# Two more attention units by rows, and another spread of the W_o products and second-norm steps over the slots of an iteration

## The chip, the cores and the metric

The kernel runs on one core of one Trainium2 chip. The metric is the device time of one execution in microseconds (us), median of several runs. Engines: PE (TensorE, matmuls), PEld (its weight loads), ACT (ScalarE), DVE (VectorE), POOL (GpSimd), SP (SyncE, which here only issues DMAs).

## The reference

One transformer block on x of 2048 x 512 (batch 1, bf16), with shift, scale and gate vectors from a small conditioning product:

```python
mod = (_silu(c) @ w_mod).reshape(c.shape[0], 6, 1, -1)       # sa, ca, ga, sb, cb, gb
h = _layernorm(x) * (1 + ca) + sa
x = x + ga * attention(h)      # 32 query heads, 8 key/value heads of 128, 2048 cached keys
h = _layernorm(x) * (1 + cb) + sb
x = x + gb * mixer(h)          # gelu(h @ w_in), spatial product over the 2048 rows, gate, w_out
```

The attention is `softmax((h @ wq) k^T / sqrt(128)) v` for every head, then `@ wo`; four query heads share one key/value head (a group). The first norm, the projections and the mixer are small beside the two attention products.

## The kernel before

**Units.** The attention is cut into 128 units (`NU`): unit u is group `u // 16` and tile `u % 16` of 128 rows of x, with the four heads of the group. Every unit has four pieces of work.

- Scores and exponential (`qk`), in iteration u of the main loop. An iteration has eight slots. In each slot PE makes 128 x 1024 scores in one of two PSUM buffers (`s_ps`, two matmuls of 512 columns) and ACT exponentiates them into SBUF.
- Times v (`pv`, `pv_rows`), in iteration `pv_at(u)`.
- Times W_o (`wo_proj`), four matmuls of 512 columns, in iteration `wo_at(u)`; DVE drains them from a PSUM buffer `misc` (two exist, shared with the query projections) and adds them into the tile's `xacc`.
- For the last group (units 112 to 127) the second norm of the finished tile (`ln2`).

**By columns or by rows.** By columns (L1029, L1036) the keys lie on the partitions, the exponentials come out as the stationary operand of the product with v, which then takes 64 matmuls of 129 columns (L1085; the last column sums the softmax's denominator). The result is normalised and transposed by a DMA (`turn`, L1108). By rows (L1010, L1017) the queries lie on the partitions; ACT also sums each row (an accumulator read after each exponential), a DMA transposes each head's 128 x 2048 exponentials into `pT` (`turn_rows`, L1049), and the product with v takes 16 matmuls of 512 columns (L1064). Its result needs no transpose, but each of the four W_o products is drained on its own (L1135), scaled by its head's denominator. The row exponentials lie in six SBUF buffers (three of them in the place of `win_sb`, which is loaded when the last row unit is through).

```python
TURN_A, TURN_B = 2 * CT, NU - CT * 2 - 1     # 8 and 119
LAGS = (2, 3, 1)
def by_rows(u):
    return TURN_A <= u < TURN_B and (u - TURN_A) % len(LAGS) < len(LAGS) - 1
```

So from unit 8 on two of three units go by rows, the third by columns. `LAGS` gives the iterations between a unit's scores and its product with v: 2 and 3 for the two row units, 1 for a column unit, which makes one such product per iteration. `wo_at` adds 3 more, or 2 for the last units.

**The order in a slot** is written out by hand, and each engine works in that order: first what `at(iteration, slot, fn)` has put there (transposes, norm steps, loads), then `qk`, then an eighth of the product with v, then query projections for later units (`fill`: one matmul in each of slots 0 to 3 in most iterations), then a W_o product. W_o products take the last slots:

```python
if i >= NSLOT - len(wf):
    wf[i - NSLOT + len(wf)]()
```

With four of them these are slots 4 to 7; with eight (two units in one iteration) all slots. SP issues its DMAs in program order, so a transpose that waits holds back those behind it.

**Second norm.** After the last W_o product of a tile, POOL (DVE for the last four tiles) applies the gate and adds x. `ln2` then places three steps: statistics on DVE and the reciprocal root on POOL (`first`), normalisation on DVE and a DMA transpose to `xnT` (`second`, L686, L1180), four modulations on DVE into `h2Ts` (`third`, L1187). The mixer's first product (`z2_tile`) reads these tiles from iteration 128 on.

Of the kernel before, what the change touches and what calls it, by code (L numbers as in the profile page):

```python
# [575 lines left out]
def kernel(  # L576
# [23 lines left out]
    REP = HQ // HKV  # L600
# [4 lines left out]
    NT = S // P  # L605
# [4 lines left out]
    CT = 512 // P  # L610
    FC = _f_chunk(FH)
    NFHC = FH // FC
    NSLOT = NKT // 2
# [61 lines left out]
    def rstd_of(mv, n, tag):  # L675

        ve = stat.tile([P, CT], FP32, name=f"ve_{tag}")
        nc.gpsimd.tensor_scalar(
            out=ve[:, :n], in0=mv[:, :, 1], scalar1=LN_EPS, scalar2=None, op0=ALU.add
        )  # L680
        rstd = stat.tile([P, CT], FP32, name=f"rstd_{tag}")
        nc.gpsimd.tensor_tensor(out=rstd[:, :n], in0=ve[:, :n], in1=mhalf[:, :n], op=ALU.pow)
        return rstd

    def normalise(dst, src, mv, rstd):
        nc.vector.tensor_scalar(  # L686
            out=dst,
            in0=src,
            scalar1=mv,
            scalar2=rstd,  # L690
            op0=ALU.subtract,
            op1=ALU.mult,
        )

    def ln_stats(mv, j, src):
        st = stat.tile([P, 1, nc.vector.BN_STATS_DIM], FP32, name="bnst")
        nc.vector.bn_stats(out=st[:, 0, :], in_=src)  # L697
        nc.vector.bn_aggr(out=mv[:, j, :], in_=st[:])
# [97 lines left out]
    def ln1_stats(j0, n):  # L796
        for j in range(j0, j0 + n):
            ln_stats(mv1, j, x_sb[:, j, :])
        return rstd_of(mv1[:, j0 : j0 + n, :], n, "ln1")
# [161 lines left out]
    first = dict(r1=ln1_stats(1, 1))  # L961


    NU = HKV * NT


    TURN_A, TURN_B = 2 * CT, NU - CT * 2 - 1

    LAGS = (2, 3, 1)

    def by_rows(u):
        return TURN_A <= u < TURN_B and (u - TURN_A) % len(LAGS) < len(LAGS) - 1
# [3 lines left out]
    def pv_at(u):  # L976
        return u + (LAGS[(u - TURN_A) % len(LAGS)] if by_rows(u) else 1)

    def wo_at(u):
        return pv_at(u) + (3 if u < NU - 6 else 2)  # L980


    users, homes = dict(pT0=-2, pT1=-1, wsp=TURN_A + 1), {}
# [8 lines left out]
    def at(it, slot, fn):  # L992
        later.setdefault((it, slot), []).append(fn)
# [173 lines left out]
    def ln2(it, j):  # L1167

        st = {}

        def first():
            if j < NT - CT:
                ln_stats(mv2, j, x_sb[:, j, :])
            st["rstd"] = rstd_of(mv2[:, j : j + 1, :], 1, "ln2")

        def second():
            xn = res.tile([P, D], BF16, name="xn2", bufs=2)
            normalise(xn[:], x_sb[:, j, :], mv2[:, j, 0:1], st["rstd"][:, 0:1])
            st["xnT"] = res.tile([P, NDT, P], BF16, name="xnT2", bufs=2)
            nc.sync.dma_start_transpose(out=st["xnT"][:], in_=xn[:])  # L1180

        def third():
            ch, c0 = j // CT, (j % CT) * P
            if ch not in h2Ts:
                h2Ts[ch] = res.tile([P, NDT, 512], BF16, name="hT", bufs=NCH)
            for dt in range(NDT):
                nc.vector.tensor_scalar(  # L1187
                    out=h2Ts[ch][:, dt, c0 : c0 + P],
                    in0=st["xnT"][:, dt, :],
                    scalar1=modc[:, 4 * NDT + dt : 4 * NDT + dt + 1],  # L1190
                    scalar2=modc[:, 3 * NDT + dt : 3 * NDT + dt + 1],
                    op0=ALU.mult,
                    op1=ALU.add,
                )

        at(it + 1, 0 if j >= NT - CT else 3, first)
        at(it + 1, 4 if j >= NT - CT else 5, second)
        at(it + 2, 5, third)

    mod_b = {}  # L1200

# [81 lines left out]
    def set_fill(b):  # L1283


        hole = TURN_A + 1 if (TURN_A + 1) // CT == b - 1 else None
        fs = qproj(b, list(range(REP)), 0, 512)
        for k, fn in enumerate(fs):
            it, slot = (b - 1) * CT + k // NDT, k % NDT
            if hole:  # L1290
                if k < NDT:
                    it, slot = hole - 1, k
                elif k < 3 * NDT:
                    it, slot = hole, k - NDT
                else:
                    it, slot = hole + 1, k - 3 * NDT
            if b == 1:
                it, slot = 2 + (10 + k) // 16, (5 + k // 2) % 8
            elif b == 2:
                it, slot = (5, k // 2) if k < 8 else (it, slot)  # L1300
            fill.setdefault((it, slot), []).append(fn)
# [8 lines left out]
    for g in range(1, HKV):  # L1310
        it = (g - 1) * NT
# [84 lines left out]
    def zrun(n):  # L1396
        for _ in range(min(n, len(zq))):
            zq.pop(0)()
# [13 lines left out]
    def pv_part(u, i, n):  # L1412
        if by_rows(u):
            return pv_rows(u, i, n)
        for k in range(NSLOT // n):
            pv(u, i * (NSLOT // n) + k)

    for it in range(NU + 6):
        if it < NU:
            if it % CT == 0 and it // CT + 1 < NB:  # L1420
                set_fill(it // CT + 1)
        elif it == NU:
            free_a.close()
            z2p = fast.enter_context(tc.tile_pool(name="z2p", bufs=1))
            zs["z2"] = z2p.tile([P, NT, FH], BF16, name="z2")
        pvs = [u for u in range(max(it - 5, 0), min(it, NU)) if pv_at(u) == it]
        wos = [u for u in range(max(it - 8, 0), min(it, NU)) if wo_at(u) == it]
        wf = [fn for u in wos for fn in wo_proj(u)]
        for i in range(NSLOT):
            for fn in later.pop((it, i), []):  # L1430
                fn()
            if it < NU:
                qk(it, i)
            if len(pvs) == 1:
                pv_part(pvs[0], i, NSLOT)
            elif pvs:
                n = NSLOT // 2
                pv_part(pvs[i // n], i % n, n)
            for fn in fill.pop((it, i), []):
                fn()  # L1440
            if i >= NSLOT - len(wf):
                wf[i - NSLOT + len(wf)]()
            if it >= NU:
                zrun(3)
        for u in wos:
            if u >= (HKV - 1) * NT:
                ln2(it, u % NT)
        if it == NU + 2:
            free_b.close()
            mlp = fast.enter_context(tc.tile_pool(name="mlp", bufs=1, side="right"))  # L1450
            zs["z1T"] = mlp.tile([P, NFT, S], BF16, name="z1T")
            wout_sb = mlp.tile([P, NFT, D], BF16, name="wout_sb")
            bsp_bc = mlp.tile([P, S], BF16, name="bsp_bc")
            nc.sync.dma_start(out=wout_sb[:], in_=wout_dram)
            nc.sync.dma_start(out=bsp_bc[:], in_=B_b_sp.partition_broadcast(P))
# [177 lines left out]
```

## Time and profile before

| | |
|---|---|
| median of 3 runs | 1308.32 us (1308.19 to 1308.85) |
| the profiled execution | 1308.74 us, span 1306.8 us |
| granted TensorE clock | 1.0 |
| DMA, share of 16 engines | 83.1% (mostly row transposes) |

The profile page gives the busy time of each engine as a share of the span. Below it are groups of equal instructions (line, engine, operation, output and inputs, shape, count; busy time and mean duration; idle time of the engine before them and who ended it). A timeline row has the start in us from the span's beginning, the duration of one instruction or of several merged ones, the engine, the line, the operation, the count, and in brackets the idle time before it with the instruction that ended it. Matmuls overlap in the pipeline: a row of one 512-column matmul says 0.38 us, while the next starts 0.22 us later, so PE's pace is read from starts.

### The profile page before, as it was taken

Reading aid. Unit: us, or ns where it says so; the run is one execution under the profiler, and the core shown is the slowest. Engines: PE = TensorE matmul, PEld = TensorE weight load, DVE = VectorE, ACT = ScalarE, POOL = GpSimd, SP = SyncE. Lnnn points to the kernel's source line nnn. Section 1 sums busy time; section 2 is a strip of 40 time slices with the busy share of each in tenths; the row PEclk is TensorE's granted clock in tenths of the full one; section 3 lists DMA queues with packets and bytes.
Section 4 is the critical chain, followed back from the end, with each engine's and each line's share of the span. In section 5 each row is a group of like instructions: output and inputs, shape, how many; then the busy total and the mean of one; then the engine's idle time right before and its main releaser. Section 6 shows DMA issues by size and latency. Waiting matters only on the chain.

```text
span 1306.8 us, 22904 instructions
## 1 busy us (share of the span) xinstructions
PE 1298.8 (99%) x8809; PEld 705.7 (54%) x8809; DVE 674.7 (52%) x1740; ACT 1113.5 (85%) x1653; POOL 56.6 (4%) x92
## 2 busy tenths in 40 slices
PE   9999999999999999999999999999999999999998
PEld 5665555555555555555555555555555566644445
DVE  5534445544554455445544554455455657694443
ACT  7899999999999999999999999999999988650000
POOL 1000000000000000000000000000000134210000
PEclk9999999999999999999999999999999999999999
DMA  7469999999999999999999999999999921364300
GB/s 183 125 127 188 163 193 183 190 168 187 189 188 168 192 168 195 177 170 186 189 189 170 187 189 179 180 188 174 182 187 171 166 82 29 57 137 98 78 20 31
DMA packets 743878, 203.33 MB, mean 156 GB/s; under 512 B 728144, under 2 KB 742608, under 8 KB 743760
## 3 DMA queue, kind: packets, MB, share of 16 engines
q1 hardware_dynamic: 741168, 199.55, 83.1%
q10 hardware_dynamic: 2592, 2.23, 0.6%
q8 instruction: 71, 1.16, 0.4%
q14 instruction: 47, 0.39, 0.1%
HBM read 21.37 MB, written 2.10 MB: 18 GB/s over the span
## 4 chain that ended last, share of the span: by engine, by line
PE 92%; DVE 0%; issue 0%
PE o_ps L1064 20%; PE s_ps L1010 19%; PE o_ps L1085 13%; PE s_ps L1029 12%; PE misc L1142 8%; PE misc L946 8%; PE misc L1500 7%; PE s_ps L1335 2%; PE s_ps L1374 2%; PE o_ps L1533 1%; PE s_ps L1533 0%; PE o_ps L856 0%; DVE xacc L1135 0%; DVE tmp L1545 0%; DVE bnst L697 0%; DVE qT L957 0%
## 5 line engine op out<-in xcount | busy, mean ns | idle before, releaser
L1010 PE MATMUL s_ps<-kT,qT 128*128 128x512 bf16 x1184 | 352.1, 379 | 0.2 <-ACT pn L1017 0.2
L1017 ACT ACTIVATE win_sb<-s_ps 128x1024 bf16<-128x1024 f32 x298 | 305.1, 1024 | 3.1 <-ACT win_sb L1017 0.5
L1036 ACT ACTIVATE pT<-s_ps 128x1024 bf16<-128x1024 f32 x256 | 258.8, 1026 | 16.8 <-PE s_ps L1029 4.8
L1064 PE MATMUL o_ps<-pT,v 128*128 128x512 bf16 x896 | 265.8, 379 | 0.0
L1029 PE MATMUL s_ps<-qT,kT 128*128 128x512 bf16 x864 | 256.8, 379 | 0.3 <-ACT pT L1036 0.2
L1135 DVE SCALAR_TENSOR_TENSOR xacc<-misc,rall,xacc 128x512 f32<-128x512 f32 x290 | 217.1, 749 | 55.5 <-PE misc L1142 49.3
L1017 ACT ACTIVATE pn<-s_ps 128x1024 bf16<-128x1024 f32 x196 | 200.7, 1025 | 1.2
L1142 PE MATMUL misc<-wo_g,oT 128*128 128x512 bf16 x512 | 194.0, 379 | 0.6 <-DVE qT L957 0.6
L1064 PEld LDWEIGHTS <-v 128*128 128x128 bf16 x1184 | 115.8, 98 | 139.7
L1036 ACT ACTIVATE wsp<-s_ps 128x1024 bf16<-128x1024 f32 x176 | 179.5, 1024 | 13.4 <-PE s_ps L1029 5.6
L946 PE MATMUL misc<-hT,wq_g 128*128 128x512 bf16 (+2 forms) x528 | 190.7, 371 | 0.1
L1010 PEld LDWEIGHTS <-qT 128*128 128x128 bf16 x1184 | 115.5, 98 | 103.9 <-issue 0.7
L1085 PEld LDWEIGHTS <-pT 128*128 128x128 bf16 x2048 | 136.8, 98 | 59.0
L957 DVE CAST qT<-misc 128x512 bf16<-128x512 f32 x127 | 87.2, 687 | 156.5 <-PE misc L946 156.4
L1085 PE MATMUL o_ps<-v,pT 128*128 128x129 bf16 x2048 | 157.2, 220 | 0.0
L1053 DVE TENSOR_TENSOR tot<-rs 128x1 f32<-128x1 f32 x296 | 46.3, 157 | 165.4 <-ACT win_sb L1017 110.1
L1029 PEld LDWEIGHTS <-kT 128*128 128x128 bf16 x864 | 83.6, 98 | 86.6 <-issue 1.8
L1085 PEld LDWEIGHTS <-wsp 128*128 128x128 bf16 x1408 | 94.3, 98 | 41.5
L1085 PE MATMUL o_ps<-v,wsp 128*128 128x129 bf16 x1408 | 108.5, 220 | 0.0
L1017 ACT ACTIVATE wmod_a<-s_ps 128x1024 bf16<-128x1024 f32 x98 | 100.3, 1024 | 0.3 <-ACT wmod_a L1017 0.3
L1500 PE MATMUL misc<-wsp,z 128*128 128x512 bf16 (+2 forms) x560 | 100.5, 336 | 0.0
L1064 PE MATMUL o_ps<-wsp,v 128*128 128x512 bf16 x288 | 85.7, 379 | 0.0
(107 smaller groups left out, 861.0 us busy)
## 6 DMA issues: line engine op xcount, KB each, us to landing
wo_g<-in_A_wo_dram SPq DMA_DIRECT2D x8, 512.0 KB, 4.7
wq_g<-in_A_wq_dram SPq DMA_DIRECT2D x7, 512.0 KB, 4.4
v<-in_A_v_cache_dram SPq DMA_DIRECT2D x7, 512.0 KB, 4.8
wsp<-in_w_mod_dram SPq DMA_DIRECT2D x1, 2048.0 KB, 8.8
out_dram<-yout ACTq DMA_DIRECT2D x16, 128.0 KB, 1.7
pT<-win_sb SPq DMA_TRANSPOSE x113, 4.8
win_sb<-in_B_w_in_dram SPq DMA_DIRECT2D x1, 1792.0 KB, 7.4
x_sb<-in_A_x_dram SPq DMA_DIRECT2D x3, 512.0 KB, 5.6
```

What stands on the lines that cost most here:

```text
L946: nc.tensor.matmul(ps[0][:, o0 : o0 + n], lhsT=wqs[g][:, dt, hh * DH : (hh + 1) * DH], rhs=hTs[ch][:, dt, c0 : c0 + n], start=(dt == 0), s ...
L957: nc.vector.tensor_copy(out=dst, in_=src)
L1010: nc.tensor.matmul(s_ps[:, c * 512 : (c + 1) * 512], lhsT=qTs[b][:, hh, jj * P : (jj + 1) * P], rhs=groups[g]["kT"][:, k0 : k0 + 512], sta ...
L1017: nc.scalar.activation(out=rows_of(u, hh)[:, half * HK : (half + 1) * HK], in_=s_ps[:], func=ACT.Exp, scale=inv_sqrt_dh, accum_out=rsums[u ...
L1029: nc.tensor.matmul(s_ps[:, h * 512 : (h + 1) * 512].rearrange("p (r q) -> p r q", r=REP), lhsT=groups[g]["kT"][:, kt * P : (kt + 1) * P], ...
L1036: nc.scalar.activation(out=pTs[u][:, 2 * i : 2 * i + 2, :], in_=s_ps[:].rearrange("p (k q) -> p k q", k=2), func=ACT.Exp, scale=inv_sqrt_dh,)
L1053: nc.vector.tensor_tensor(out=tot[:], in0=rs[:, 2 * hh : 2 * hh + 1], in1=rs[:, 2 * hh + 1 : 2 * hh + 2], op=ALU.add)
L1064: nc.tensor.matmul(o_pss[u][:], lhsT=groups[g]["v1"][:, kt, 0:DH], rhs=pTs[u][:, kt, :], start=(kt == 0), stop=(kt == NKT - 1),)
L1085: nc.tensor.matmul(o_ps[:, hh % 2, 0 : DH + 1], lhsT=pTs[u][:, kt, hh * P : (hh + 1) * P], rhs=groups[g]["v1"][:, kt, 0 : DH + 1], start=( ...
L1135: nc.vector.scalar_tensor_tensor(out=xa[:], in0=X_ps[:], scalar=scale, in1=xa[:], op0=ALU.mult, op1=ALU.add)
L1142: nc.tensor.matmul(ps[0][:], lhsT=oTs[u][:, hh, :], rhs=groups[g]["wo"][:, hh, :], start=(hh == 0 or each), stop=(hh == REP - 1 or each),)
L1500: nc.tensor.matmul(g_pss[f][:, :n], lhsT=z2[:, st, f * P : (f + 1) * P], rhs=wsp[t][:, st, c0 : c0 + n], start=(st == 0), stop=(st == NT - ...
```

## The change

Three parts. `TURN_B` becomes 122, so units 119 and 120 go by rows and 121 closes the pattern by columns; the load of `win_sb`, tied to `TURN_B`, moves from iteration 120 to 123, and the iteration with two products with v from 120 to 123. The W_o delay of 3 instead of 2 iterations now holds for units 122 to 124 too. Iterations with four W_o products put them into slots 0, 2, 4, 6; those with eight use all slots as before, and are now iterations 126 (units 120 and 122) and 128 (124 and 125) instead of 123 (117 and 119) and 125 (121 and 122). The three steps of the second norm move to slots 2 (0 for the last four tiles), 4 and 3.

```diff
-    TURN_A, TURN_B = 2 * CT, NU - CT * 2 - 1
+    TURN_A, TURN_B = 2 * CT, NU - 6
...
     def wo_at(u):
-        return pv_at(u) + (3 if u < NU - 6 else 2)
+        return pv_at(u) + (3 if u < NU - 3 else 2)
...
-        at(it + 1, 0 if j >= NT - CT else 3, first)
-        at(it + 1, 4 if j >= NT - CT else 5, second)
-        at(it + 2, 5, third)
+        at(it + 1, 0 if j >= NT - CT else 2, first)
+        at(it + 1, 4, second)
+        at(it + 2, 3, third)
...
-            if i >= NSLOT - len(wf):
-                wf[i - NSLOT + len(wf)]()
+            if len(wf) > REP:
+                wf[i]()
+            elif wf and i % 2 == 0:
+                wf[i // 2]()
```

## The prediction

> **What bounds the kernel now.** I read the page first (shares of busy time), then the timeline of PE and ACT in iterations 8 to 13, 62 to 65 and 116 to 127, then the SP queue. An iteration of the main loop has eight slots; from iteration 8 on three kinds alternate: A and B exponentiate by rows, C by columns (119 is an A, 120 a B, 121 a C if the pattern goes on).
>
> ```profile
> PE 1298.8 (99%) x8809; PEld 705.7 (54%) x8809; DVE 674.7 (52%) x1740; ACT 1113.5 (85%) x1653; POOL 56.6 (4%) x92
> L1085 PEld LDWEIGHTS <-pT 128*128 128x128 bf16 x2048 | 136.8, 98 | 59.0
> ```
>
> PE is busy throughout, so the test is its pace. The PE timeline gives the starts of iterations 62 (A), 63 (B) and 65:
>
> ```profile
> 547.68 0.59 PE L1010 MATMUL s_ps<-kT,qT 128*128 128x512 bf16 x2
> ...
> 556.49 0.59 PE L1010 MATMUL s_ps<-kT,qT 128*128 128x512 bf16 x2
> ...
> 573.75 0.59 PE L1010 MATMUL s_ps<-kT,qT 128*128 128x512 bf16 x2
> ```
>
> A takes 8.81 us, B and C together 17.26, so 8.63 each. B holds 40 products of 512 columns: 0.2158 us from start to start, with no gap. A holds the 64 products of 129 columns of a column unit in place of 16 long ones: 0.0567 us each. The main loop runs at PE's own pace; from start to start the whole trace holds only some 8 us beyond that pace, about 5 of them before 20 us and few later.
>
> What can make PE wait is the pair of score buffers: the scores of slot i+2 go where ACT has read slot i. The PE timeline of iteration 12 (no W_o there, so two slots have only four products), then ACT's:
>
> ```profile
> 117.99 0.59 PE L1010 MATMUL s_ps<-kT,qT 128*128 128x512 bf16 x2
> 118.42 0.59 PE L1064 MATMUL o_ps<-pT,v 128*128 128x512 bf16 x2
> 118.85 0.59 PE L1010 MATMUL s_ps<-kT,qT 128*128 128x512 bf16 x2
> ...
> 121.01 0.59 PE L1010 MATMUL s_ps<-kT,qT 128*128 128x512 bf16 x2
> ```
> ```profile
> 118.67 1.02 ACT L1017 ACTIVATE win_sb<-s_ps 128x1024 bf16<-128x1024 f32 x1
> 119.59 0.19 ACT L1017 ACTIVATION_READ_ACCUMULATOR win_sb<-s_ps 128x1 f32 x1
> 119.68 1.02 ACT L1017 ACTIVATE win_sb<-s_ps 128x1024 bf16<-128x1024 f32 x1
> ...
> 121.70 1.02 ACT L1017 ACTIVATE wmod_a<-s_ps 128x1024 bf16<-128x1024 f32 x1
> ```
>
> A four-product slot lasts 0.86 us (117.99 to 118.85). A fresh row exponential starts 0.68 to 0.69 after its scores do (118.67; 121.01 to 121.70). The next cannot start sooner than 1.01 later (118.67 to 119.68), so a 0.86 slot leaves ACT behind. When it frees the buffer, iteration 9 shows, where ACT is the limit (ACT, then PE):
>
> ```profile
> 91.42 1.02 ACT L1017 ACTIVATE pn<-s_ps 128x1024 bf16<-128x1024 f32 x1
> 92.33 0.20 ACT L1017 ACTIVATION_READ_ACCUMULATOR pn<-s_ps 128x1 f32 x1
> ```
> ```profile
> 92.58 0.59 PE L1010 MATMUL s_ps<-kT,qT 128*128 128x512 bf16 x2 [0.20 <-ACT pn L1017]
> ```
>
> The exponential ends at 92.44, the accumulator read at 92.53, the waiting scores start at 92.58: 0.14 after the exponential ends. A row exponential thus needs 1.02 + 0.14 = 1.16 us from its start to the reuse of its buffer; a column one has no accumulator read.
>
> **The change, part by part.** Times are against the profiled execution, 1308.74 us with a span of 1306.8; the median of the runs is 1308.32, so a difference is carried over to that.
>
> *Two units more by rows (119, 120).* PE: 16 x 0.2158 = 3.45 for 64 x 0.0567 = 3.63, 0.18 less for each, **-0.35 us**. ACT is slower per row exponential, but 1.08 a slot of PE covers 1.00, as in the 37 pairs before. On DVE four W_o products of each are drained one by one (L1135, 749 ns); the old pattern does the same without a wait.
>
> *W_o in slots 0, 2, 4, 6 instead of 4 to 7.* No product more or less, but the slots become uneven. Old B: eight of 1.079. New B: 1.295, 1.079, 1.295, 1.079, 1.079, 0.863, 1.079, 0.863 (query products stay in 0 to 3). Follow ACT in B: slot 5 fresh, 0.69 after its scores; slot 6: 0.69 + 1.01 - 0.86 = 0.84; buffer free at 0.84 + 1.16 = 2.00 after the scores of slot 6; PE wants it after slots 6 and 7, 1.08 + 0.86 = 1.94. PE waits 0.06. In A the short slots are 0.885: 0.69 + 1.01 - 0.885 = 0.815, free at 1.975, wanted at 1.985: no wait, by 0.01. In C the column exponentials can follow each other in 0.90 (their spacing in iteration 4, where ACT is the limit) and have no accumulator read: no wait. B iterations with this pattern: 15, 18, ... 120, that is 36: 36 x 0.06 = **+2.1 us**, with PE as the bound all of it on the path.
>
> The Trainium skill ("ScalarE: Activation LUTs", section "What ACT_TABLE_LOAD costs") says that an activation with immediate scale and bias takes 186 ns + 0.833 ns per element and that those back to back overlap by about 93 ns, an estimate of 0.95 us for 1,024 elements; by it slot 6 would free its buffer in time and this term would be nil. The rows with an accumulator read disagree: 1.01, and 1.00 once behind.
>
> *What the even spread repairs.* Iteration 11 (no query products; row exponentials against four slots of 0.885) runs from 105.46 to 113.67, 8.21 for a PE sum of 7.94; with W_o in every second slot a pair of slots is 1.985 and the same sum gives no wait: -0.27. Iterations 4, 124, 126, 127 likewise lose 0.08 and three times 0.06: -0.25. Iteration 9 is short of PE work either way (waits of 0.46 now, 0.55 by the same recurrence): +0.1. Together **-0.4 us**.
>
> *The double W_o iteration.* Units 117 and 119 both project in iteration 123 today, together with query products that hold a bank:
>
> ```profile
> 1087.61 0.62 PE L1085 MATMUL o_ps<-v,pT 128*128 128x129 bf16 x8
> 1088.80 0.38 PE L1142 MATMUL misc<-wo_g,oT 128*128 128x512 bf16 x1 [0.57 <-DVE qT L957]
> ```
>
> The product was due at 1087.61 + 8 x 0.057 = 1088.07 and starts 0.73 late; another at 1083.02 is 0.16 late. In the new order the doubles are in 126 and 128, which have no query products: **-0.9 us**.
>
> *Second norm.* Statistics one slot earlier (3 to 2), normalisation and its transpose on SP 5 to 4, modulation 5 to 3. Nothing is added; DVE has slack (52% busy), and PE needs only its drained banks. Behind a waiting DVE stand the drains, due about 0.7 to 1 us before PE would notice. The statistics wait for POOL (1.27 + 1.17); the last W_o product also comes a slot earlier, so cover shifts with need. The modulation waits for xnT: issued at 1036.91 in iteration 118, now ahead of one row transpose, some 2.6 us earlier, landing (2.7 median) near 1037.1 with the modulation at 1037.7. Cost nothing; up to 1 us if one is late.
>
> *SP queue.* The normalised tile's transpose (1.2 to 1.6 us of issue) now stands among the four transposes of unit 119, needed two iterations on. For unit 116:
>
> ```profile
> 1027.51 3.44 SPq L1049 DMA_TRANSPOSE pT<-wmod_a x1
> ...
> 1036.91 1.57 SPq L1180 DMA_TRANSPOSE xnT<-xn x1
> ```
> ```profile
> 1034.87 0.38 PE L1064 MATMUL o_ps<-pT,v 128*128 128x512 bf16 x1
> ```
>
> Last transpose issued at 1027.51, 5.0 median to land, used at 1034.87: 2.4 to spare, less 0.4 (heads finish later in the new slots) and 1.6: 0.4 left. Nothing, or up to 1 us once. The win_sb load moves from iteration 120 to 123; it takes 7.4 us and is first read about 40 us later. W_o of 120 is two iterations later, of 119 and 122 to 124 one; their normalised tiles are read two iterations after they are ready at the latest.
>
> Sum: -0.35 + 2.1 - 0.4 - 0.9 = **+0.5 us**: 1308.8 for the median.
>
> **The rivals.** (1) *No wait in B*: the buffer is freed sooner than worked out, for example because slot 5's exponential starts 0.63 after its scores, as in column units. Then -1.65: 1306.7. Against it: 121.70. (2) *Slower*: the first exponential after a fresh one comes more than 1.01 later in the uneven slots. With x more, B pays 0.06 + x and A, whose margin is 0.01, pays x - 0.01: 36 x (0.05 + 2x) - 1.65. Over 0.2% (2.6 us, about what a measurement of this kernel can tell from no change) from x = 0.035; at x = 0.05 it is +3.75: 1312.1. For it: A's margin is nearly nothing, and in iteration 117 an ACT start is 0.28 late for no reason in the slots; against it, 1.01 is the same in 9, 11 and 12. (3) *Unit 119's transposes late*: +1 once, 1309.8. (4) *Weight loads bind the column products*: if each took its 98 ns in turn, a column unit would cost 64 x 0.098 = 6.27 and each conversion save 2.8: 1303.5, faster. Against it: 0.0567 from start to start, and A only 0.18 longer than B. The Trainium skill ("TensorE: Matmul & The Clock Gate", section "Back-to-back issue gap") gives sustained 81 ns at N=128 and 131 ns at N=512, by which two conversions would save some 6 us; this trace has 57 and 216.
>
> **How the numbers follow.** Forecast 0.58, (1) 0.14, (2) 0.14, (3) 0.12, (4) 0.02. Faster: only (4), since all repairs together are 1.65 us, 0.13%. Slower: (2). The rest is within 0.2%. The range goes from (1), 1306.6, to (2) at x = 0.035, 1311.2, which leaves out (4) and most of (2).
>
> **What would show it.** Right: in the new trace B iterations of 8.69 (C's first scores 0.06 late, released by ACT), A at 8.81, iteration 11 at 7.95, no 0.73 gap near 1088. Wrong: B at 8.63 (rival 1), A longer than 8.83 (rival 2), a PV of iteration 121 released by a DMA (rival 3), or PE waits on DVE at L1142 in the steady part, which I price at nothing.

## The result

The changed kernel takes 1311.15 us (median of 16 runs, 1310.58 to 1311.70) where the kernel before takes 1308.38 (16 runs, 1307.88 to 1309.11): 2.77 us more, ratio 1.0021, 95% interval 1.0014 to 1.0028. The forecast was 1308.8, with a range of 1306.6 to 1311.2. The profiled execution has a span of 1309.6 us, 2.74 more than before, and a granted clock of 1.0.

The page's line of engines:

```profile
PE 1300.1 (99%) x8713; PEld 700.9 (54%) x8713; DVE 695.7 (53%) x1756; ACT 1094.7 (84%) x1669; POOL 57.2 (4%) x92
```

The 96 matmuls fewer are the two conversions (2 x (64 - 16)). Shares of busy time say nothing more; the starts of iterations 62 (A), 63 (B), 64 (C) and 65 (A) in the PE timeline do:

```profile
549.90 0.59 PE L1010 MATMUL s_ps<-kT,qT 128*128 128x512 bf16 x2
...
558.71 0.59 PE L1010 MATMUL s_ps<-kT,qT 128*128 128x512 bf16 x2
...
566.48 0.59 PE L1010 MATMUL s_ps<-kT,qT 128*128 128x512 bf16 x2
566.91 0.59 PE L1064 MATMUL o_ps<-wsp,v 128*128 128x512 bf16 x2
567.40 0.59 PE L1029 MATMUL s_ps<-qT,kT 128*128 128x512 bf16 x2
...
576.03 0.59 PE L1010 MATMUL s_ps<-kT,qT 128*128 128x512 bf16 x2
```

A still lasts 8.81 (549.90 to 558.71) and C 8.63 (567.40 to 576.03), while B lasts 8.69 (558.71 to 567.40). Slot 7 of B should take 0.86, as slot 5 does, and takes 0.92 (566.48 to 567.40). ACT, end of the same B:

```profile
565.23 1.02 ACT L1017 ACTIVATE win_sb<-s_ps 128x1024 bf16<-128x1024 f32 x1
...
566.24 1.02 ACT L1017 ACTIVATE win_sb<-s_ps 128x1024 bf16<-128x1024 f32 x1
567.15 0.20 ACT L1017 ACTIVATION_READ_ACCUMULATOR win_sb<-s_ps 128x1 f32 x1
```

The exponential of slot 6 starts 1.01 after that of slot 5, and the waiting scores at 567.40 start 1.16 after it: the recurrence of the prediction in its two constants.

Where the other time went is read from the same starts, kernel against kernel (us more than before, summed over the span):

| part of the span | change |
|---|---|
| before iteration 0 (differs from run to run: -0.60 to +0.18 in other profiles) | +0.13 |
| iteration 4 | -0.09 |
| iteration 5 | **+0.94** |
| iteration 9 | **+0.39** |
| iteration 11 | -0.26 |
| iterations 15 to 120: 36 B at 0.057, the rest of them slightly shorter | +1.92 |
| 21 and 117 (B) beyond the 0.057, not in the row above | **+0.56** |
| iteration 120 (without its B wait) to the last matmul | -1.41 |
| after the last matmul's start | **+0.57** |

The four bold rows, 2.46 together, have no counterpart in the prediction except 0.1 for iteration 9. Iteration 5, a column unit's, where nothing was expected (PE, then DVE):

```profile
55.96 0.62 PE L1085 MATMUL o_ps<-v,pT 128*128 128x129 bf16 x8
57.35 0.59 PE L946 MATMUL misc<-hT,wq_g 128*128 128x512 bf16 x2 [0.78 <-DVE qT L957]
```
```profile
55.83 0.66 DVE L697 BATCH_NORM_STATS2 bnst<-x_sb 128x6 f32<-128x512 bf16 x1
56.53 0.18 DVE L698 BATCH_NORM_AGGREGATE mv<-bnst 128x2 f32<-128x6 f32 x1
56.63 0.67 DVE L957 CAST qT<-misc 128x512 bf16<-128x512 f32 x1
```

A query product, due at 55.96 + 8 x 0.057 = 56.42, starts at 57.35, when DVE has drained the bank of the query product before (56.63 + 0.67 = 57.30). In the kernel before PE went straight from one to the other:

```profile
55.70 0.62 PE L1085 MATMUL o_ps<-v,pT 128*128 128x129 bf16 x8
56.16 0.59 PE L946 MATMUL misc<-hT,wq_g 128*128 128x512 bf16 x2
```

There the same cast came later still, from 56.97 to 57.64, but the product did not need it: it had the other bank. The reason is in `wo_proj`: for a column unit `bank("misc")` is called at the first of its four W_o products only, which add up in that bank. With the products in slots 4 to 7 the bank is held to the end of the iteration; with slots 0, 2, 4, 6 from its start. Iterations 5 and 9 project the queries of two heads, and while one `misc` bank is held these have only the other, so each waits for the cast of the one before. In iteration 5 the cast stands behind norm statistics on DVE (0.66 to 0.68 each), in 9 it does not:

```profile
93.77 0.59 PE L1010 MATMUL s_ps<-kT,qT 128*128 128x512 bf16 x2
94.50 0.38 PE L946 MATMUL misc<-hT,wq_g 128*128 128x512 bf16 x1
```
```profile
93.75 0.69 DVE L957 CAST qT<-misc 128x512 bf16<-128x512 f32 x1 [0.44 <-PE misc L946]
```

Scores at 93.77, and the next product not 0.43 but 0.73 later: 0.30.

At the place that answers to the gap near 1088 there is now none (1088.43 + 16 x 0.057 = 1089.34):

```profile
1088.43 1.07 PE L1085 MATMUL o_ps<-v,pT 128*128 128x129 bf16 x16
1089.34 0.38 PE L1142 MATMUL misc<-wo_g,oT 128*128 128x512 bf16 x1
```

### The profile page after: what moved, and what is told of

Read it like the earlier page. It is cut to its first block, busy times and chain, and to the rows that moved or that the text cites. A ratio compares the mean times of both kernels' runs of the same rounds, so it can differ in the third digit from the quotient of the medians.

```text
span 1309.6 us, 22627 instructions
## 1 busy us (share of the span) xinstructions
PE 1300.1 (99%) x8713; PEld 700.9 (54%) x8713; DVE 695.7 (53%) x1756; ACT 1094.7 (84%) x1669; POOL 57.2 (4%) x92
## 3 DMA queue, kind: packets, MB, share of 16 engines
q8 instruction: 70, 1.15, 0.4%
## 4 chain that ended last, share of the span: by engine, by line
PE 98%; DVE 1%; DMA 0%; ACT 0%; issue 0%; SPq 0%; DVEq 0%; ACTq 0%
PE o_ps L1064 20%; PE s_ps L1010 20%; PE o_ps L1085 14%; PE s_ps L1029 14%; PE misc L1142 8%; PE misc L946 8%; PE misc L1502 7%; PE s_ps L1335 2%; PE s_ps L1374 2%; PE o_ps L1535 1%; DMA wmod_a<-in_w_mod_dram 0%; PE s_ps L1535 0%; DVE bnst L697 0%; DVE qT L957 0%; ACT win_sb L1017 0%; DVE hT L815 0%
## 5 line engine op out<-in xcount | busy, mean ns | idle before, releaser
L1010 PE MATMUL s_ps<-kT,qT 128*128 128x512 bf16 x1216 | 361.6, 379 | 0.1
L1017 ACT ACTIVATE win_sb<-s_ps 128x1024 bf16<-128x1024 f32 x306 | 312.1, 1024 | 10.6 <-PE s_ps L1010 8.7
L1135 DVE SCALAR_TENSOR_TENSOR xacc<-misc,rall,xacc 128x512 f32<-128x512 f32 x298 | 223.6, 750 | 150.0 <-PE misc L1142 140.6
L1064 PE MATMUL o_ps<-pT,v 128*128 128x512 bf16 x912 | 271.2, 379 | 0.0
L1029 PE MATMUL s_ps<-qT,kT 128*128 128x512 bf16 x832 | 247.2, 379 | 0.4 <-ACT pT L1036 0.2
L1036 ACT ACTIVATE wsp<-s_ps 128x1024 bf16<-128x1024 f32 x160 | 161.6, 1024 | 9.6 <-PE s_ps L1029 5.1
L1029 PEld LDWEIGHTS <-kT 128*128 128x128 bf16 x832 | 79.8, 98 | 86.6 <-issue 7.7
L1085 PEld LDWEIGHTS <-wsp 128*128 128x128 bf16 x1280 | 85.7, 98 | 37.8
L1085 PE MATMUL o_ps<-v,wsp 128*128 128x129 bf16 x1280 | 98.7, 220 | 0.0
L1064 PE MATMUL o_ps<-wsp,v 128*128 128x512 bf16 x304 | 89.8, 379 | 0.0
```

The source lines that it names most:

```text
L1010: nc.tensor.matmul(s_ps[:, c * 512 : (c + 1) * 512], lhsT=qTs[b][:, hh, jj * P : (jj + 1) * P], rhs=groups[g]["kT"][:, k0 : k0 + 512], sta ...
L1017: nc.scalar.activation(out=rows_of(u, hh)[:, half * HK : (half + 1) * HK], in_=s_ps[:], func=ACT.Exp, scale=inv_sqrt_dh, accum_out=rsums[u ...
L1029: nc.tensor.matmul(s_ps[:, h * 512 : (h + 1) * 512].rearrange("p (r q) -> p r q", r=REP), lhsT=groups[g]["kT"][:, kt * P : (kt + 1) * P], ...
L1036: nc.scalar.activation(out=pTs[u][:, 2 * i : 2 * i + 2, :], in_=s_ps[:].rearrange("p (k q) -> p k q", k=2), func=ACT.Exp, scale=inv_sqrt_dh,)
L1064: nc.tensor.matmul(o_pss[u][:], lhsT=groups[g]["v1"][:, kt, 0:DH], rhs=pTs[u][:, kt, :], start=(kt == 0), stop=(kt == NKT - 1),)
L1085: nc.tensor.matmul(o_ps[:, hh % 2, 0 : DH + 1], lhsT=pTs[u][:, kt, hh * P : (hh + 1) * P], rhs=groups[g]["v1"][:, kt, 0 : DH + 1], start=( ...
```

## The experiments

**Each part alone.** Theory: the slots cost, the rows and the double iteration gain, and the cost is the larger. `rows_only` is the changed kernel with the old slot code and the old three `at(...)` of `ln2`; `slots_only` and `norm_only` are the kernel before with one part each:

```diff
 # slots_only
-            if i >= NSLOT - len(wf):
-                wf[i - NSLOT + len(wf)]()
+            if len(wf) > REP:
+                wf[i]()
+            elif wf and i % 2 == 0:
+                wf[i // 2]()
 # norm_only
-        at(it + 1, 0 if j >= NT - CT else 3, first)
-        at(it + 1, 4 if j >= NT - CT else 5, second)
-        at(it + 2, 5, third)
+        at(it + 1, 0 if j >= NT - CT else 2, first)
+        at(it + 1, 4, second)
+        at(it + 2, 3, third)
```

> Only the two further row units and the later W_o iterations; W_o products stay in slots 4 to 7, the second norm where it was. Theory (ACT's lag in uneven slots costs; the row units and the moved double iteration gain): the conversion gives 0.3 to 0.35 us, the wait of 0.9 us in iteration 123 goes, nothing else: 1307.1 us, 1.2 below the kernel before, and no PE wait for ACT in iterations 15 to 120. Rival (the two further row units themselves cost, through their transposes or drains): at or above the kernel before, with PE waits in iterations 119 to 123.

> Only the W_o products of iterations with four of them move to slots 0, 2, 4, 6; row units end at 118 as before, the second norm is where it was. Theory: 35 waits of 0.057 us in the second row iterations (2.0), 0.6 more in iterations 21 and 117, 0.94 in iteration 5 and 0.39 in iteration 9 where query products and a column unit's W_o share two banks, less 0.26 in iteration 11, 0.09 in 4 and 0.17 in 124 to 127; the double iteration 123 keeps its 0.9: about 3.4 us above the kernel before, 1311.8. Rival (the loss comes of the norm steps or of the further row units): no more than 1 us above.

> Only the three steps of the second norm move to slots 2, 4, 3. Theory: DVE has room and PE waits for none of it: within 0.3 us of the kernel before. Rival (DVE blocked behind a late transpose or a late POOL step holds up W_o drains): 0.5 to 2 us above, with PE waits for DVE at the W_o products of iterations 117 to 131.

Measured, against 1308.40: rows 1307.76 (0.9995, 0.9986 to 1.0004), slots 1311.37 (1.0023, 1.0014 to 1.0032), norm 1309.24 (1.0007, 0.9998 to 1.0016). The intervals are about 0.1% to either side, 1.2 us, so the times alone tell only the slots from no change. Smaller effects, here and below, are read from the loops in the traces, where kernels that share a loop agree to 0.005 us. From iteration 0 to the last matmul the traces give -1.15, +3.11 and +0.89; the changed kernel has +2.04. Rows and slots alone add up to 1.96, so all but 0.08 of the norm's cost is missing in the full change. It is in two places of iterations 121 and 123; the first, PE then DVE of `norm_only`:

```profile
1069.90 0.62 PE L1085 MATMUL o_ps<-v,wsp 128*128 128x129 bf16 x8
1070.83 0.38 PE L1142 MATMUL misc<-wo_g,oT 128*128 128x512 bf16 x1 [0.30 <-DVE qT L957]
```
```profile
1067.86 0.70 DVE L697 BATCH_NORM_STATS2 bnst<-x_sb 128x6 f32<-128x512 bf16 x1 [2.62 <-POOL x_sb L1159]
...
1068.68 0.95 DVE L1187 TENSOR_SCALAR hT<-xnT,modc 128x128 bf16<-128x128 bf16 x4
...
1070.09 0.68 DVE L957 CAST qT<-misc 128x512 bf16<-128x512 f32 x1
```

DVE waits 2.62 for POOL, then does statistics and modulation ahead of the cast that frees a bank (in the kernel before it waits as long there, but the modulation stands behind the cast). My term of nothing for the norm (a drain due 0.7 to 1 us early) does not hold there; in the changed kernel the W_o products of these iterations come in other slots, and PE does not wait there. In the loop, the slots are nearly the whole cost.

The conversion and the double iteration were forecast at -1.25; the loop shows -1.15. The median shows less because the end of the program is longer, see below.

**The slots of B.** All three are the changed kernel with another choice of slots for four products:

```diff
-            elif wf and i % 2 == 0:
-                wf[i // 2]()
+            wo_slots = ...
+            elif wf and i in wo_slots:
+                wf[wo_slots.index(i)]()
```

with (0, 4, 5, 6) in B in `b_one_short` (only slot 7 is short at the end), (0, 2, 4, 5) in `b_two_adjacent` (6 and 7 short), (4, 5, 6, 7) in `b_old_slots`, and (0, 2, 4, 6) elsewhere.

> The changed kernel, but in the second row iterations (15, 18, ... 120) the W_o products are back in slots 4 to 7. Theory: the 36 waits of 0.057 us for ACT go, and with them the 0.6 us in iterations 21 and 117: 2.6 us below the changed kernel, about 1308.5. Rival (ACT's lag is only where the time shows, and PE waits elsewhere instead): less than 1 us below the changed kernel.

> The changed kernel, but in the second row iterations the W_o products stand in slots 0, 4, 5, 6, so that one slot of 1.295 us follows one of 0.863. Theory: with one short slot ACT's lag of 0.15 us is never wanted back in time, no wait: 2.3 to 2.6 us below the changed kernel. Rival (any early W_o product, drained in slots 0 to 3, costs): half of the gain or less.

> The changed kernel, but in the second row iterations the W_o products stand in slots 0, 2, 4, 5, so that the two short slots, 6 and 7, follow each other. Theory: the buffer of slot 6 is free 0.68 + 1.02 + 0.14 = 1.85 after its scores, PE wants it after 0.863 + 0.863 = 1.73: a wait of 0.12 us in each of 36 iterations in place of 0.057, so 2.3 us above the changed kernel. Rival (what counts is only how many short slots there are, or how late the last drain is): the same time as the changed kernel.

Measured: `b_one_short` 1308.78, 2.37 less than the changed kernel, with no wait in B but 0.12 in each of 21 and 117. `b_two_adjacent` 1312.96, 1.81 more where 2.3 was expected; its loop is 2.15 longer, with 0.12 per B in place of 0.057, as expected, but nothing more in 21 and 117. The term reacts to the spacing of short slots as the recurrence says.

`b_old_slots` missed: 1319.77 (1.0087), slower by 8.6 instead of faster. ACT's waits in B are gone, but a new one stands in slot 0 of every C behind such a B (PE, then DVE, iteration 16):

```profile
149.74 0.38 PE L946 MATMUL misc<-hT,wq_g 128*128 128x512 bf16 x1
150.26 0.38 PE L1142 MATMUL misc<-wo_g,oT 128*128 128x512 bf16 x1
```
```profile
148.86 0.69 DVE L1073 CAST oT<-o_ps 128x512 bf16<-128x512 f32 x1
149.47 0.74 DVE L1135 SCALAR_TENSOR_TENSOR xacc<-misc,rall,xacc 128x512 f32<-128x512 f32 x1
```

B's last W_o product in slot 7 and C's first in slot 0 are neighbours now; the bank is drained at 150.21, and the product due 0.22 after 149.74 starts 0.52 after it. 36 x 0.31 = 11.1, less 2.6, is 8.5. A mixed order of slots is a third kernel, not a half of two.

**Iterations 5 and 9.** `early_old_slots` puts the old slots there: `wo_slots = (4, 5, 6, 7) if it in (5, 9) else (0, 2, 4, 6)`.

> The changed kernel, but iterations 5 and 9, which have two heads of query products, keep W_o in slots 4 to 7. Theory: a column unit's four W_o products fill one bank, held from slot 0 to slot 6 in the changed kernel, which leaves the query products one; with slots 4 to 7 the 0.94 us wait in iteration 5 goes and iteration 9 is back at 8.10 us: 1.3 us below the changed kernel. Rival (the wait is DVE's own lateness): less than 0.5 us below.

Measured 1310.40, 0.75 less than the changed kernel, expected 1.3. The 0.94 of iteration 5 is gone, and 0.29 of iteration 9; but slot 7 again meets slot 0 of the next iteration, and iterations 6 and 10 lose 0.16 and 0.24 waiting for the drain of the column sum (L1127). The cause of iteration 5 stands, the repair is partial.

**The late exponential in 21 and 117.** Both show one slot 5 that starts late (ACT, iteration 21 of the changed kernel, then PE):

```profile
199.46 1.02 ACT L1017 ACTIVATE win_sb<-s_ps 128x1024 bf16<-128x1024 f32 x1 [0.25 <-ACT win_sb L1017]
```
```profile
200.21 0.38 PE L1142 MATMUL misc<-wo_g,oT 128*128 128x512 bf16 x1
200.62 0.59 PE L1010 MATMUL s_ps<-kT,qT 128*128 128x512 bf16 x2
201.05 0.59 PE L1064 MATMUL o_ps<-wsp,v 128*128 128x512 bf16 x2
201.63 0.59 PE L1029 MATMUL s_ps<-qT,kT 128*128 128x512 bf16 x2
```

It comes 1.37 after that of slot 4 where the other B have 1.09, and PE then waits twice, 0.19 ahead of 200.62 and 0.14 ahead of 201.63. The kernel before has the same late start in the same slot (and both have one in slot 7 of iteration 80); there no PE wait follows. `after_act_shift` adds 12 small activations early:

```diff
+    es = res.tile([P, NDT], FP32, name="es")
+    for _ in range(12):
+        nc.scalar.activation(out=es[:], in_=c_f[:], func=ACT.Exp, scale=-1.0)
```

> The changed kernel with 12 more small activations (128x8, into a tile that nothing reads) on ACT in the start-up, so that every ACT instruction of the loop stands 12 places later in ACT's stream. In the changed kernel one exponential in slot 5 of iteration 21 and one in 117 start 0.28 us late though their scores are there, and those two iterations are 0.28 longer than the other B iterations. Theory (tied to a place in ACT's stream, about 1664 instructions apart): the late starts move to about 12 ACT instructions earlier in the work, that is 6 to 8 slots earlier, out of slot 5 of 21 and 117 into iterations 20 and 116 (C and B by the pattern: in 20 slack hides it); 21 and 117 then last as the other B iterations, 8.69. Rival (tied to the iteration's work, for example to what DVE or a queue does there): still 0.28 late in slot 5 of 21 and 117. The whole time differs by at most 0.6 either way, with the start-up's own cost on top (the activations take some 0.2 us each there).

Measured 1310.75 (1.0019, 1.0009 to 1.0028). The same exponential in its iteration 21 (the lines of this kernel are 3 further on):

```profile
198.60 1.02 ACT L1020 ACTIVATE win_sb<-s_ps 128x1024 bf16<-128x1024 f32 x1
```

No idle time ahead of it, and likewise in 117. Late starts of 0.25 to 0.28 stand instead in slot 7 of 35 and slot 5 of 72, not in 20 and 116 as I expected; 72 is a B and pays 0.28. So the loop is 0.28 shorter (1.76 over before, in place of 2.04). The late start belongs to a place in ACT's program, not to the iteration's work.

The traces show more of the place. Counted over all of ACT's recorded instructions from the first on, waits included, the late exponentials are numbers 320, 1344 and 1984 in each of the twelve kernels without the extra activations, and 576 and 1216 with them. All are 64 more than a multiple of 128, and each stands right behind a wait. In the thirteen traces no exponential right behind a wait at another number of this series exists, and those at a multiple of 128 (512 and 1152 in the changed kernel) are on time. With the extra activations number 320 is an accumulator read, in slot 0 of iteration 21, so no exponential is late there. The DMA records also have 47 or 48 loads of 8,192 bytes of instructions in an execution, one in some 27 us; after each of the 38 late starts of the thirteen traces the next one begins within 0.6 to 2.3 us. That the late start is a step from one loaded stretch of the program to the next is argued from this, not shown.

**The end of the program.** From the last matmul to the end of the span it is 5.71 us before and 6.28 after, though DVE's and ACT's work there is the same. In the trace SP ends the program by waiting for eight DMA semaphores one after the other, twice, some 0.07 each; DMAs use these in rotation. The changed kernel issues six DMAs more (eight row transposes, less two of `oT`), and the last output falls on the first of the eight instead of the third. `after_three_loads` adds two DMAs, by loading `win_sb` in three parts:

```diff
-    at(TURN_B + 1, 2, lambda: nc.sync.dma_start(out=win_sb, in_=win_dram))
+    def load_win():
+        for a, b in ((0, 1), (1, 2), (2, NDT)):
+            nc.sync.dma_start(out=win_sb[:, a:b], in_=win_dram[:, a:b])
+
+    at(TURN_B + 1, 2, load_win)
```

> The changed kernel, with the load of win_sb in iteration 123 issued as three DMAs instead of one, so that SP issues two DMAs more: 8 more than the kernel before instead of 6. The loop is the same. Theory (the end of the program): from the last matmul's start to the end of the span the kernel before takes 5.71 us and the changed one 6.28, and every kernel so far with TURN_B = 122 takes 6.0 to 6.3, because SP waits one after the other for eight DMA semaphores that are used in rotation, and the last output's landing falls on the first of them, so all eight waits come after it; with 8 more DMAs the rotation stands as before, two or three of the waits are over before the landing, and the end takes 5.65 to 5.75: 0.4 to 0.6 less, 1310.7, with the loop unchanged to 0.1. Rival (the end is chance, or the landing itself): it stays at 6.0 to 6.3, and the time at 1311.2.

Times from the last matmul's start, from the traces (us):

| kernel | SP's waits over before the last output lands | it lands | end of the span | from landing to end |
|---|---|---|---|---|
| before | 2 | 3.85 | 5.71 | 1.86 |
| changed | 0 | 3.91 | 6.28 | 2.37 |
| `after_three_loads` | 2 | 3.66 | 5.84 | 2.18 |

Measured 1310.72 (1.0018, 1.0009 to 1.0027), 0.43 less than the changed kernel, with the loop the same to 0.002 us. The rotation is as said, and is worth 0.19 from landing to end. The other traces agree: from landing to end it is 2.37 in all eight kernels with 513 DMAs, 2.18 in both with 515, and 1.79 to 1.92 in the three with 507. The other 0.32 of the 0.51 is a gap of 0.35 between two of SP's waits, which stays. It is not chance either: it stands in all ten kernels with the further row units, each time right ahead of SP's 873rd recorded instruction, and in the other three SP's program ends with the 869th. What SP does in the gap is not shown. When the output lands differs between profiles (3.65 to 3.96), so the rest of the 0.43 cannot be given to one cause.

**The spread only where it costs nothing.** `spread_where_free` keeps the rows, the old steps of the norm and the old slots, with (0, 2, 4, 6) only in 4, 11 and 124 to 127; `spread_three_loads` has the three loads as well.

```diff
+            wo_slots = (0, 2, 4, 6) if it in (4, TURN_A + 3) or NU - CT <= it < NU else (4, 5, 6, 7)
```

> Row units until 121 and the later W_o iterations; W_o in slots 0, 2, 4, 6 only in iterations without query products (4, 11, 124, 125, 127), in slots 4 to 7 elsewhere; the second norm where it was. Theory: the gains without the waits: 0.3 conversion, 0.9 from iteration 123, 0.26 from 11, 0.09 from 4, 0.1 to 0.2 from 124 to 127: 1306.7 us, 1.7 below the kernel before. Rival (gains in single iterations are taken back by a later one): no faster than the kernel with the row units alone.

> The version with the even spread only where it costs nothing, again with win_sb's load as three DMAs. That version gave 1307.16, ratio 0.9991, with 0.3 to 0.5 lost at the end of the program. Theory (semaphore rotation): the end shrinks to 5.65 to 5.75 from the last matmul, and the time to 1306.7, ratio 0.9987. Rival (chance): 1307.2.

Measured 1307.16 (0.9991, 0.9982 to 1.0000) and 1306.83 (0.9988, 0.9979 to 0.9997). The loop of both is 1.73 shorter than before, as expected; the end takes part of that back. The second is the fastest kernel of this study, 1.6 us under the kernel before.

## Why the prediction was right or wrong

*Conversion and double iteration, -0.35 and -0.9: right together*, -1.15 in the loop of `rows_only`; the two were not run apart. The rival in which weight loads bind is out with it: two conversions bring nothing like 5.6.

*W_o slots in B, +2.1: right in cause, place and size.* 36 x 0.057 = 2.0, with 0.12 where two short slots end B and nothing where one does. The rival without a wait is out. In the rival on the other side x is nil: 1.01 in B, and A stays at 8.81 with its margin of 0.01. B's row, 1.01 from start to start, decided against the estimate from the Trainium skill ("ScalarE: Activation LUTs", section "What ACT_TABLE_LOAD costs"): by 0.95 no B would wait.

*Even spread, -0.4: right for 11, 4 and 124 to 127* (-0.26, -0.09, -0.22), *wrong for 9*, +0.39 in place of +0.1. There I carried the recurrence of ACT over and did not look at banks.

*W_o products of iteration 5: missing from the sum*, 0.94. The sentence "PE needs only its drained banks" stood under the second norm and was weighed for steady iterations, which project one head's queries. That a column sum holds a bank from its first product to its last, and that I had moved its first product four slots ahead, is in `wo_proj`; the two-head iterations are in `fill`.

*A late ACT start: named, and priced only as a rival.* The prediction cites the one in iteration 117 for its second rival. The start is no lengthening of every slot; it costs where a B's slack is gone, 0.28 twice.

*Second norm, nothing: right in this kernel, wrong alone* (+0.89 in the loop). *SP queue, nothing: right*; the last of unit 119's transposes lands at 1064.23, 0.28 ahead of its first use at 1064.52 (0.4 forecast), so the third rival is out, narrowly. *The end of the program* had no term: 0.51.

So the forecast missed by 2.35 us, nearly all of it outside the term that it spent most words on: 0.94, 0.3, 0.56 and 0.5. That 1311.15 still lies inside the range, by 0.05 us, is luck: the upper end, 1311.2, was the second rival at x = 0.035, and x is nil; costs that the sum did not have brought the time there.

## What to carry to other kernels

When a matmul that adds up in a PSUM bank is moved earlier, price the bank from its first product to its last drain, in the odd iterations at the start too, not only in the steady one. Before mixing an old order with a new one, look at the seam: the last slot of one iteration beside the first of the next. Where a change takes the slack of a repeated step, search the trace before for rare late starts that this slack hides now.

## What was not expected of the hardware

One exponential in some hundreds starts 0.25 to 0.28 us late with its input ready and its engine idle, at the same numbers of ACT's recorded instructions in each kernel (five numbers, multiples of 128 apart); 12 instructions put ahead of the loop gave these places to other work. And the number of DMAs alone, through the semaphore that the last one falls on, moves the end of the program by 0.19 us.
